# Loading the second x tile through ScalarE's DMA queue, and transposing it inside the first V group

## The chip, the cores and the metric

One core of a Trainium2 chip runs the whole kernel in one launch. The metric is the device time of an execution in microseconds (us). The *span* of a trace runs from the core's first instruction to its last; in these runs the time is the span plus 1.8 us (1.75 to 1.86), save in e13 and e17, where it is the span plus 1.83 to 2.11, for a reason that no run shows. A group of kernels measured together shares one chip and the runs of the kernel before on it; different groups ran on different chips.

The 2% that would count as faster or slower is 14 us.

## The reference, cut to what matters

A transformer block on x of 2048 x 1024 in bf16: LayerNorm, sliding-window attention of width 256 with 32 heads, then LayerNorm and a dense layer with SiLU.

```python
x = A_x
h  = x + _A_ref(_layernorm(x), A_wqkv, A_wo)      # qkv = LN(x) @ wqkv, windowed softmax, @ wo
h2 = h + _B_ref(_layernorm(h), B_w1, B_w2)        # silu(LN(h) @ w1) @ w2
return h2
```

Only the first 25 us matter to the change: LayerNorm of the first four x tiles (x0 to x3, 128 rows each) and the V projection of these rows.

## The kernel before

SyncE issues all loads in this order; each `load_wqkv` is 1 MB, each `load_x` 0.26 MB.

```python
    def load_x(b, j):
        nc.sync.dma_start(out=x_ring[(b % 2) * 4 + j], in_=x2d[(b * 4 + j) * P:(b * 4 + j + 1) * P, :])
    ...
    load_x(0, 0)
    load_wqkv(2 * D)             # V weights, columns 0 to 511
    load_x(0, 1)
    load_wqkv(2 * D + 512)       # V weights, columns 512 to 1023
    load_x(0, 2)
    load_x(0, 3)
    for c0 in (0, D, 512, D + 512):
        load_wqkv(c0)
```

A tile goes through LayerNorm on VectorE (with the root on ScalarE), is transposed on TensorE in two halves of four 128 x 128 blocks, and copied out of PSUM by ScalarE. Then a V group multiplies it: eight matmuls into one PSUM bank, and a cast of the result by ScalarE.

```python
    def turn_first(xt, dst, j):
        for h in range(2):
            for i in range(4):
                kt = h * 4 + i
                nc.tensor.transpose(out=tp_ps[h][:, i * P:(i + 1) * P], in_=xt[:, kt * P:(kt + 1) * P], identity=ident[:])
            nc.scalar.copy(out=dst[:, h * 4:(h + 1) * 4, j * P:(j + 1) * P], in_=...)
    def v_group(b, j, c, copy):
        acc = next_acc()
        for kt in range(KT):
            nc.tensor.matmul(acc, lhsT=lnT_b[b % 2][:, kt, j * P:(j + 1) * P], rhs=wv[:, kt, c * 512:(c + 1) * 512], ...)
        copy(out=v[...], in_=acc...)
    ...
    ln_first(x_ring[0], st, rs, 0)
    turn_first(x_ring[0], lnT_b[0], 0)
    ln_first(x_ring[1], st, rs, 1)
    v_group(0, 0, 0, act)
    turn_first(x_ring[1], lnT_b[0], 1)
    ln_first(x_ring[2], st, rs, 2)
    v_group(0, 1, 0, act)                 # "the second V group" below
    v_group(0, 0, 1, act)
    ...
    dummy = small.tile([P, 1], F32, name="dummy", tag="dummy")
    nc.scalar.activation(out=dummy[:], in_=eps[:], func=ACT.Exp)
```

The softmax here doesn't subtract the row's maximum and nothing guards it: scores larger than these inputs give would overflow.

## Time and profile before

| | |
|---|---|
| time known at the prediction | 699.61 us, median of 3 (699.46 to 699.77) |
| the execution that was profiled | 699.17 us, span 697.4 us |
| TensorE (PE) busy | 98% of the span |
| x1 lands | 7.28 us |
| second V group starts | 10.94 us; dense PE work from there |

The prediction below shows the lines.

### The profile page before, as it was taken

The numbers are of one execution on the slowest core, as the hardware profiler recorded it, in microseconds if no ns is written. First come the engines' busy times: TensorE is split into PE (matmuls) and PEld (weight loads), VectorE is DVE, ScalarE is ACT, GpSimd is POOL, SyncE is SP. The second block draws the span as 40 slices with busy tenths as digits, with TensorE's granted clock in tenths as the row PEclk, the third lists the DMA queues.
The fourth block names the chain that finished last, engine by engine and source line by source line (L and its number), as shares of the span: only waits on it lengthen the run. The fifth ranks groups of instructions, "written<-read, shape, count | busy, mean of one in ns | idle before, by whom it ended". The sixth has DMA issues, their size and how long they took to land.

```text
span 697.4 us, 12171 instructions
## 1 busy us (share of the span) xinstructions
PE 686.6 (98%) x4970; PEld 334.9 (48%) x5059; DVE 286.5 (41%) x608; ACT 259.9 (37%) x335; POOL 172.3 (25%) x375
## 2 busy tenths in 40 slices
PE   8999999999999999999999999999999999999998
PEld 3444555555555555544444444444444444444445
DVE  5446645753444348544425233334144251233111
ACT  4316667777777777621310023300033200233000
POOL 1006566777777777600000000000000000000000
PEclk9999999999999999999999999999999999999999
DMA  9541123025431578881023410023300024100110
GB/s 311 171 73 57 32 55 91 17 49 157 116 122 25 180 228 293 211 296 58 32 75 99 105 39 1 0 77 83 83 1 0 10 92 96 46 1 0 31 39 23
DMA packets 75399, 60.55 MB, mean 87 GB/s; under 512 B 49232, under 2 KB 59472, under 8 KB 75344
## 3 DMA queue, kind: packets, MB, share of 16 engines
q1 hardware_dynamic: 75344, 59.78, 29.7%
q8 instruction: 39, 0.64, 0.4%
q14 instruction: 16, 0.13, 0.1%
HBM read 39.85 MB, written 8.39 MB: 69 GB/s over the span
## 4 chain that ended last, share of the span: by engine, by line
PE 97%; DMA 1%; issue 1%; DVE 0%; ACT 0%; SPq 0%
PE hacc L461 18%; PE hacc L498 17%; PE acc L224 16%; PE acc L498 10%; PE acc L461 9%; PE acc L216 8%; PE acc L243 7%; PE o_ps L297 5%; PE sc L261 4%; PE hacc L243 2%; DMA r_o<-in_A_x_dram 1%; PE o_ps L196 0%; DVE ln_st L158 0%; ACT r_w L197 0%; DVE r_o L179 0%
## 5 line engine op out<-in xcount | busy, mean ns | idle before, releaser
L272 ACT ACTIVATE r_e<-sc 128x1024 bf16<-128x1024 f32 (+2 forms) x192 | 175.8, 967 | 66.1 <-PE sc L261 52.5
L287 POOL TENSOR_SCALAR_AFFINE_SELECT r_e<-r_e 128x256 bf16<-128x256 bf16 (+1 forms) x368 | 169.3, 489 | 120.7 <-ACT r_e L272 117.7
L498 PEld LDWEIGHTS <-r_a 128*128 128x128 bf16 x952 | 90.9, 98 | 103.0
L461 PEld LDWEIGHTS <-r_w 128*128 128x128 bf16 x896 | 87.4, 98 | 104.8
L498 PE MATMUL hacc<-r_a 128*128 128x512 bf16 (+2 forms) x605 | 121.9, 359 | 0.6
L461 PE MATMUL hacc<-r_e,r_w 128*128 128x512 bf16 x444 | 100.2, 379 | 0.6
L470 ACT ACTIVATE r_n<-hacc 128x512 f32<-128x512 f32 x30 | 17.9, 597 | 178.9 <-PE hacc L461 178.9
L224 PEld LDWEIGHTS <-r_w 128*128 128x128 bf16 x512 | 46.1, 98 | 58.6 <-issue 8.9
L498 PE MATMUL acc<-r_a 128*128 128x512 bf16 x328 | 73.6, 379 | 0.4
L226 DVE CAST r_a<-acc 128x512 bf16<-128x512 f32 x56 | 38.7, 691 | 81.3 <-PE acc L224 57.7
L297 PEld LDWEIGHTS <-r_e 128*128 128x128 bf16 x1440 | 50.3, 96 | 22.7
L224 PE MATMUL acc<-r_t,r_w 128*128 128x512 bf16 x240 | 60.0, 380 | 0.8
L224 PE MATMUL acc<-r_w 128*128 128x512 bf16 x246 | 57.7, 380 | 0.5
L297 PE MATMUL o_ps<-r_a,r_e 128*128 128x33 bf16 x1440 | 51.2, 178 | 0.0
L243 PE MATMUL acc<-r_o,r_a 128*128 128x512 bf16 x196 | 48.7, 380 | 0.6
L461 PE MATMUL acc<-r_e,r_w 128*128 128x512 bf16 x216 | 49.1, 379 | 0.0
L243 PEld LDWEIGHTS <-r_a 128*128 128x128 bf16 x256 | 23.1, 98 | 29.6 <-issue 5.1
L261 PE MATMUL sc<-r_a 32*128 32x128 bf16 (+2 forms) x704 | 37.2, 276 | 0.0
L513 DVE SCALAR_TENSOR_TENSOR r_t<-hacc,r_t 128x512 bf16<-128x512 f32 (+2 forms) x22 | 14.0, 635 | 56.4 <-PE hacc L498 56.4
L513 DVE SCALAR_TENSOR_TENSOR r_t<-acc,r_t 128x512 bf16<-128x512 f32 x12 | 8.3, 692 | 64.2 <-PE acc L498 59.7
L471 DVE SCALAR_TENSOR_TENSOR r_a<-r_n,hacc 128x512 bf16<-128x512 f32 x30 | 20.6, 688 | 33.0 <-ACT r_n L470 33.0
L461 PE MATMUL hacc<-r_a,r_w 128*128 128x512 bf16 x141 | 32.7, 379 | 0.2
(65 smaller groups left out, 419.7 us busy)
## 6 DMA issues: line engine op xcount, KB each, us to landing
r_w<-in_B_w_dram SPq DMA_DIRECT2D x8, 896.0 KB, 5.2
r_a<-in_B_w_dram SPq DMA_DIRECT2D x7, 1024.0 KB, 7.8
r_w<-in_A_wqkv_dram SPq DMA_DIRECT2D x6, 1024.0 KB, 11.3
r_o<-in_A_x_dram SPq DMA_DIRECT2D x16, 256.0 KB, 4.2
h_dram<-r_t SPq DMA_DIRECT2D x16, 256.0 KB, 3.2
r_t<-h_dram SPq DMA_DIRECT2D x16, 256.0 KB, 2.8
out_dram<-r_t SPq DMA_DIRECT2D x31, 128.0 KB, 1.7
r_e<-h_dram SPq DMA_DIRECT2D x3, 1024.0 KB, 5.7
```

Source lines behind the costliest of these rows:

```text
L216: nc.tensor.matmul(acc, lhsT=lnT_b[b % 2][:, kt, j * P:(j + 1) * P], rhs=wv[:, kt, c * 512:(c + 1) * 512], start=(kt == 0), stop=(kt == KT ...
L224: nc.tensor.matmul(acc, lhsT=wqk[:, kt, col0:col0 + P], rhs=lnT_b[b % 2][:, kt, :], start=(kt == 0), stop=(kt == KT - 1))
L226: copy(out=(qT, kT)[which][b][:, g, :], in_=acc)
L243: nc.tensor.matmul(acc, lhsT=qT[b][:, g, j * P:(j + 1) * P], rhs=wo[:, g, c * 512:(c + 1) * 512], start=(g == 0), stop=(g == G - 1))
L261: nc.tensor.matmul(sc[hh // 2][:, hh % 2, ch * P:(ch + nq) * P], lhsT=kT[t // 4][r0:r0 + DH, g, (t % 4) * P:(t % 4 + 1) * P], rhs=qT[b][r0 ...
L272: nc.scalar.activation(out=e[:, :, lo:hi], in_=sc[pair][:, :, lo:hi], func=ACT.Exp, scale=scale)
L287: nc.gpsimd.affine_select(out=ap, in_=ap, pattern=[[0, 2], [0, n], [sgn, P]], compare_op=ALU.is_ge if upper else ALU.is_gt, fill=0.0, base ...
L297: nc.tensor.matmul(o_ps[pair][:, qt * 2 + hh, 0:VW], lhsT=e_of(i, kind, pair)[:, hh, ch * P:(ch + 1) * P], rhs=v[:, b * 4 + kt, g * 4 + pa ...
L461: nc.tensor.matmul(acc, lhsT=w1[:, kt, ft * P:(ft + 1) * P], rhs=ln2T[b][:, kt, :], start=(kt == 0), stop=(kt == KT - 1))
L471: nc.vector.scalar_tensor_tensor(out=gT[:, ft, :], in0=th, scalar=1.0, in1=acc, op0=ALU.add, op1=ALU.mult)
L498: nc.tensor.matmul(acc[:, 0:c1 - c0], lhsT=gT[:, ft, j * P:(j + 1) * P], rhs=w2[ft // 4][:, ft % 4, c0:c1], start=(ft == 0), stop=(ft == F ...
L513: nc.vector.scalar_tensor_tensor(out=t_out[j % 2][:, c0:c1], in0=acc[:, 0:c1 - c0], scalar=0.5, in1=t_in[j % 2][:, c0:c1], op0=ALU.mult, o ...
```

## The change

Intent: get x1 to VectorE before the first megabyte of V weights, and give PE half a V group to do while x1 is normalized. A dummy Sqrt loads ScalarE's function table first.

```diff
-    def load_x(b, j):
-        nc.sync.dma_start(...)
+    def load_x(b, j, queue=nc.sync):
+        queue.dma_start(...)
...
+    eps = const.tile([P, 1], F32, name="eps")
+    nc.vector.memset(eps[:], LN_EPS)
+    dummy = const.tile([P, 1], F32, name="dummy")
+    nc.scalar.activation(out=dummy[:], in_=eps[:], func=ACT.Sqrt)
+
     load_x(0, 0)
     load_wqkv(2 * D)
-    load_x(0, 1)
+    load_x(0, 1, nc.scalar)
...
-    def v_group(b, j, c, copy):
+    def v_group(b, j, c, copy, between=None):
         acc = next_acc()
         for kt in range(KT):
+            if between and kt in between:
+                between[kt]()
...
-    v_group(0, 0, 0, act)
-    turn_first(x_ring[1], lnT_b[0], 1)
+    v_group(0, 0, 0, act, {4: lambda: turn_first(x_ring[1], lnT_b[0], 1, (0,)),
+                           6: lambda: turn_first(x_ring[1], lnT_b[0], 1, (1,))})
...
-    dummy = small.tile([P, 1], F32, name="dummy", tag="dummy")
     nc.scalar.activation(out=dummy[:], in_=eps[:], func=ACT.Exp)
```

More of the change, by code (lines that the diff above doesn't have):

```diff
@@ L123 @@
     w2_v = B_w2.rearrange("(ft p) n -> p ft n", p=P)
-    def load_x(b, j):
-        nc.sync.dma_start(out=x_ring[(b % 2) * 4 + j], in_=x2d[(b * 4 + j) * P:(b * 4 + j + 1) * P, :])
+    def load_x(b, j, queue=nc.sync):
+        queue.dma_start(out=x_ring[(b % 2) * 4 + j], in_=x2d[(b * 4 + j) * P:(b * 4 + j + 1) * P, :])
     def load_wqkv(c0):
@@ L143 @@
     make_identity(nc, ident[:])
-    eps = const.tile([P, 1], F32, name="eps")
-    nc.vector.memset(eps[:], LN_EPS)
     warm = ebuf[0]
@@ L190, in ln_first, with turn_first @@
             ln_norm(xt[:, h * 512:(h + 1) * 512], st, rs, j)
-    def turn_first(xt, dst, j):
-        for h in range(2):
+    def turn_first(xt, dst, j, halves=(0, 1)):
+        for h in halves:
             for i in range(4):
```

## The prediction

> **What bounds the kernel now.** I read the page first, for who is the bound, then the chain of waits cut to the first 40 us, then the timeline of the first 25 us, and last the DMA queue by stretches, because the change touches nothing after about 11 us.
>
> The page, busy time by engine and the chain that ended last:
>
> ```profile
> span 697.4 us, 12171 instructions
> ...
> PE 686.6 (98%) x4970; PEld 334.9 (48%) x5059; DVE 286.5 (41%) x608; ACT 259.9 (37%) x335; POOL 172.3 (25%) x375
> ...
> PE 97%; DMA 1%; issue 1%; DVE 0%; ACT 0%; SPq 0%
> ```
>
> TensorE is the bound over the whole span. Only 697.4 - 686.6 = 10.8 us of it are idle, so a change that doesn't shorten the matmuls can win only part of that. The one non-PE item of any size on the chain is "DMA", 1%. The chain of waits in the first 40 us tells where it lies (start, length, what):
>
> ```profile
> 1.73 5.55 DMA r_o<-in_A_x_dram
> 7.28 0.02 issue
> 7.30 1.30 DVE ln_st L158 x2
> ...
> 9.40 0.42 DVE r_o L179
> 9.82 0.05 issue
> 9.87 0.41 PE o_ps L196 x4
> 10.28 0.02 issue
> 10.30 0.59 ACT r_w L197
> 10.89 0.05 issue
> 10.94 3.19 PE acc L216 x14
> ```
>
> So the start is set by the second x tile (x1): issued third on SyncE's queue at 1.73, behind x0 and the first megabyte of V weights, landed at 7.28, then LayerNorm, transposes, copy, and from 10.94 on the chain is PE alone. The timeline shows the same stretch from PE's and DVE's side (start, length, engine, instruction, idle before):
>
> ```profile
> 0.80 1.28 ACT L187 ACT_TABLE_LOAD   x1 [0.80 <-PEq L535]
> ...
> 3.70 1.29 DVE L158 BATCH_NORM_STATS2 ln_st<-r_o 128x6 f32<-128x512 bf16 x2 [2.20 <-DMA r_o<-in_A_x_dram]
> ...
> 5.79 0.74 DVE L179 TENSOR_SCALAR r_o<-r_o,st_a,rs_a 128x512 bf16<-128x512 bf16 x2
> ...
> 7.30 1.29 DVE L158 BATCH_NORM_STATS2 ln_st<-r_o 128x6 f32<-128x512 bf16 x2 [0.78 <-DMA r_o<-in_A_x_dram]
> ...
> 7.33 1.90 PE L216 MATMUL acc<-r_w 128*128 128x512 bf16 x8 [0.36 <-ACT r_w L197]
> ...
> 9.87 0.72 PE L196 MATMUL o_ps<-ident,r_o 128*128 128x128 bf16 x8 [0.63 <-DVE r_o L179]
> ...
> 10.94 3.63 PE L216 MATMUL acc<-r_w 128*128 128x512 bf16 x15 [0.35 <-ACT r_w L197]
> ```
>
> Two things are to be seen. DVE is free at 5.79 + 0.74 = 6.53 and waits 0.78 us for x1: that is all that an earlier landing can give, because DVE can't start on x1 before it is done with x0. And PE idles 0.63 before the x1 transposes and 0.35 before the second V group. After that the stream is dense: 16 matmuls from 10.94 to the next transposes at 14.40 are 216 ns each; the eight transposes at 14.40 put the next group at 14.85, so eight cost 0.45 us in a dense stream.
>
> The DMA side in stretches (us, then busy of each engine, clock, DMA share, GB/s):
>
> ```profile
> 1.55:6.26 4.71, 4.25 (x11) 1.44 (x12) 2.13 (x6) 0.83 (x2) 2.08 (x1) 1.00 0.91 311
> 7.33:10.94 3.61, 2.62 (x16) 1.16 (x17) 2.37 (x6) 1.96 (x5) 0.00 (x0) 1.00 1.08 359
> 10.94:23.93 12.99, 12.88 (x70) 6.37 (x73) 4.69 (x12) 7.77 (x15) 0.00 (x0) 1.00 1.09 351
> ```
>
> The engines are saturated until about 24 us, so a second queue adds no bytes per second; it only reorders. And in the last of these stretches PE is busy 12.88 of 12.99: nothing later in the block can take back what is won before.
>
> **What the Trainium skill says.** "DMA: Bandwidth & Descriptors", section "Queues, rings and completion order": each of the 16 engines goes round its queue rows packet by packet, so x1 in its own row takes turns with V instead of standing behind it. That DMA work is bandwidth-bound here (351 to 359 GB/s) agrees with the same page's view of shared engines; that rows take turns, no view of before can show, as it has one such queue. "Perfetto Trace Analysis", section "DMA Instruction — HWDGE": the descriptor generator is shared and locked for one issue at a time, so ScalarE's issue may wait for SyncE's. Before, an unhindered issue on SyncE takes 0.40 to 0.43 us, one of an x tile at 2.83 takes 1.28, which may be such back-pressure; nothing contends yet. The same page, section "Sequencer Loop": engine instructions are pushed into a queue and others read on meanwhile. So the DMA behind the dummy Sqrt may be issued at about 1 us and not only when table load (0.80 to 2.08) and Sqrt are done; before has no case of it. "TensorE: Matmul & The Clock Gate", section "Part 1: The HAM clock gate": the clock halves after about a 3.4 us idle window. The longest gap that I foresee is under 1 us, and the granted clock of before is 1.00 in every stretch, so no clock effect.
>
> **The change part by part.**
>
> *x1's landing.* Before 7.28. Needed: by 6.5, when DVE is free. From x0 I take the plain latency: issued 0.81, landed with 3.70 at the latest, 2.9 us. If ScalarE issues at 2.3 (after table load and Sqrt, 0.20 us as the Exp dummy at 22.58 took), x1 lands uncontended at 5.2; 256 KB at half of 360 GB/s take 1.4 us in place of 0.7, so 5.9. If it issues at about 1.0 to 1.3 it lands at 4 to 5. Both are ahead of 6.5, so the exact landing doesn't matter in either.
>
> *x1's LayerNorm.* Starts at 6.5 in place of 7.30. From its start to its first transpose before was 9.87 - 7.30 = 2.57, so the first transpose now starts at about 9.07. ScalarE's root has to be at about 8.05, and ScalarE's copies of x0 end at 7.77: free.
>
> *V weights.* x1's 0.26 MB come out of the first V load's share: V landed 5.3 us after 1.27, at 6.57, and now up to 0.26 MB / 360 GB/s = 0.73 us later, 7.30. The first V group starts at 7.33 before, so this just fits; and the four matmuls ahead of the first transposes (4 x 0.216 = 0.86) need only be done by 9.07, which leaves 0.9 us of slack. The second V load and x2 have the same bytes ahead of them as before: unchanged.
>
> *PE order.* Four V matmuls 7.33 to 8.19; idle to 9.07 (0.88, worse than any one gap of before); four transposes 0.23, two matmuls 0.43, four transposes 0.23, two matmuls 0.43: 10.39. The second V group's first four matmuls need only the first half's copy, which starts near 9.5 and is done by 10.1; its second four need the second half near 11.25, copied by 10.75. So the copies, 0.59 each and 0.35 of PE idle before, are hidden. The group starts at 10.39 in place of 10.94: 0.55 us won. Of this 0.8 is the earlier LayerNorm, and 0.25 is given back because half a V group that used to run in the wait now stands behind it.
>
> *Later.* x2's transposes would come at 10.39 + 3.46 = 13.85; x2's norm ran 13.06 to 13.79 before and depends on its landing (10.95), not on PE: just in time, slack 0.1 to 0.3. From there PE is dense. The dummy Sqrt and the earlier eps memset (0.06) cost ScalarE and DVE time in which they idle.
>
> *x0.* It now may share the engines with x1 if ScalarE issues early. x0's landing heads the whole chain one for one. The DMA engines aren't full then (0.38 to 0.81 busy by stretches before 2.8 us), so I put 0.0 to 0.5 on it, 0.15 in the mean.
>
> Sum: -0.55 + 0.15 = -0.4 us, 699.61 - 0.4 = 699.2.
>
> **The rivals.**
> 1. The early issue: x1 runs abreast of x0, x0 lands up to 0.5 us later, and everything after shifts. For it: the sequencer reads on past queued work. Against it: two queues may fill the slow ramp better, and SyncE's issue is first. Time 699.4 to 699.6.
> 2. The late landing: ScalarE waits for the generator's lock while SyncE's issues are stuck (1.28 us at 2.83), or V's queued descriptors go first. The gain is gone at a landing of 7.05 and beyond it each us costs one. For it: issues of 3.4 us later in the load. Against it: V and x1 together are through by 7.28 as before. Time 699.6 to 700.2.
> 3. The whole wait vanishes: PE's 0.98 us of idle in the stretch as page readers would add it. Against it: DVE can't start before 6.5, and four matmuls no longer fill the wait. Time 698.6.
> 4. The gain is taken back: x2 becomes the wait at 13.85. Against it: it needs a landing over 0.2 us later than before. Time 699.3 to 699.5.
>
> **Range and chances.** The repeats of before spread by 0.31 us. Main branch 699.05, rival 1 and 4 699.3 to 699.6, rival 2 up to 700.2. I say 699.2, range 698.7 to 699.8. 2% is 14 us, more than the whole idle time of PE on the faster side, and no rival loses it: within 2% 0.985, faster 0.005, slower 0.01.
>
> **What would show it.** Right: x1's statistics start at about 6.5 straight behind x0's normalization with no DMA wait; one PE gap of 0.8 to 0.9 in the first V group, none before the second group, which starts near 10.4; PE dense from there and the shift unchanged at 24 us. x0's statistics still at 3.70: main branch; later: rival 1. x1's statistics waiting for DMA beyond 6.6: rival 2. A gap before x2's transposes near 13.9: rival 4. The prediction is wrong if the first x tile lands over 0.5 us later, if the time leaves 698.7 to 699.8, or if the early shift is there but the end doesn't have it.

## The result, and the profile after

The changed kernel took 698.49 us (median of 6, 698.27 to 699.01) against 699.69 us (median of 6, 699.17 to 702.72): 1.20 us between the medians. The forecast was 699.2 with a range from 698.7, so the measured time is below the range. The ratio of the fast runs is 0.9977 (95% interval 0.996 to 0.9994). Ratios here divide the mean time of one kernel's fast runs by that of the other's of the same rounds, so they are not quite the ratio of the medians, and not every ratio can be recomputed from the executions listed. This one holds an execution of before at 702.72 us, within 1.5% of the fastest and so counted as fast; without it the means are 698.53 and 699.65, a ratio of 0.9984.

The two traces differ by less than the times: spans 696.7 and 697.4 us, 0.7 apart. The timeline of the changed kernel, in the stretch that the prediction showed of before (start, length, engine, instruction, idle before):

```profile
0.80 1.28 ACT L136 ACT_TABLE_LOAD   x1 [0.80 <-PEq L539]
0.81 0.40 SPq L127 DMA_DIRECT2D r_o<-in_A_x_dram  x1
...
0.97 0.38 ACTq L127 DMA_DIRECT2D r_o<-in_A_x_dram  x1
...
3.66 1.29 DVE L161 BATCH_NORM_STATS2 ln_st<-r_o 128x6 f32<-128x512 bf16 x2 [2.16 <-DMA r_o<-in_A_x_dram]
...
6.40 1.28 DVE L161 BATCH_NORM_STATS2 ln_st<-r_o 128x6 f32<-128x512 bf16 x2
...
7.38 1.04 PE L221 MATMUL acc<-r_w 128*128 128x512 bf16 x4 [0.45 <-ACT r_w L200]
...
8.95 0.40 PE L199 MATMUL o_ps<-ident,r_o 128*128 128x128 bf16 x4 [0.53 <-DVE r_o L182]
...
9.62 0.39 PE L199 MATMUL o_ps<-ident,r_o 128*128 128x128 bf16 x4
...
9.84 4.05 PE L221 MATMUL acc<-r_w 128*128 128x512 bf16 x18
```

ScalarE issued x1 at 0.97, while its table load was still running. x1's statistics follow x0's normalization with no DMA wait, at 6.40 in place of 7.30. There is one PE gap in the first V group (0.53 us idle, where the forecast had 0.88) and none before the second. The 18 matmuls from 9.84 are the last two of the first group and the 16 of the next two, so the second V group starts two matmuls later, at 9.84 + 0.43 = 10.27 in place of 10.94. That is 0.67 us, and it is kept: the chain of waits of the changed kernel is PE alone from there.

```profile
8.48 0.42 DVE r_o L182
8.91 0.05 issue
8.95 0.40 PE o_ps L199 x4
9.35 0.43 PE acc L221 x2
9.78 0.22 PE o_ps L199 x4
10.01 3.88 PE acc L221 x18
13.89 0.45 PE o_ps L199 x8
14.34 3.45 PE acc L221 x16
```

Two questions follow: why the times differ by 1.2 when the traces differ by 0.7, and which part of the change does it.

### The profile page after: what moved, and what is told of

The parts are those of the page before. It is cut to its first block, busy times and chain, and to the rows that moved or that the text cites. A ratio compares the mean times of both kernels' runs of the same rounds, so it can differ in the third digit from the quotient of the medians.

```text
span 696.7 us, 12261 instructions
## 1 busy us (share of the span) xinstructions
PE 691.4 (99%) x5059; PEld 335.1 (48%) x5059; DVE 286.3 (41%) x608; ACT 260.0 (37%) x336; POOL 171.6 (25%) x375
## 4 chain that ended last, share of the span: by engine, by line
PE 98%; DVE 1%; DMA 0%; ACT 0%; issue 0%
PE hacc L465 19%; PE hacc L502 17%; PE acc L229 17%; PE acc L502 10%; PE acc L465 9%; PE acc L221 8%; PE acc L248 7%; PE o_ps L302 5%; PE sc L266 4%; PE hacc L248 1%; DMA r_o<-in_A_x_dram 0%; DVE ln_st L161 0%; PE o_ps L199 0%; DVE r_o L182 0%; ACT rs_a L190 0%; DVE st_a L162 0%
```

## The experiments

One relation helps to read all of them. In fourteen of the fifteen traces that run at full clock and become dense with the second V group, the span is the start of this group plus 686.4 to 686.6 us (before: 10.94 and 697.4; changed: 10.27 and 696.7). The exception is told under e12. So a tenth of a microsecond at the start is a tenth at the end, and the spans of unprofiled executions tell roughly where their second V group started.

### The kernel before again, and each half of the change alone

**e1_before_again**: no edit.

> The unchanged kernel, to get a second profile and the spread of its runs. The profiled execution of before (699.17) was the fastest of its six, the median 699.69. Theory A (the 1.2 us between the medians is the 0.68 us that the traces show in the start of the dense PE stream, and the rest is chance in which execution was profiled): a second profile shows its second V group at 10.9 to 11.4 and a span of 697.4 to 698.0, and a time over the kernel before of 1.000 within 0.0005. Theory B (before's start jitters because every delay of x1's landing goes into its path, and the change took this jitter away): its runs spread over more than 0.6 us, and x1's statistics start later than 7.30 in a slower execution.

Measured: 699.26 us (699.12 to 699.38), ratio to before 0.9997 (0.9985 to 1.001). In its trace x1's statistics start at 7.41, the second V group at 11.04, and the span is 697.5. Its own five runs spread little; the nine runs of before beside it spread from 699.18 to 699.78. Start, span and ratio are as theory A had them. Theory B's spread of over 0.6 us is not in its own runs, and is just reached in the nine.

**e2_queue_only**: the changed kernel with PE's old order.

```diff
-    v_group(0, 0, 0, act, {4: ..., 6: ...})
+    v_group(0, 0, 0, act)
+    turn_first(x_ring[1], lnT_b[0], 1)
```

> x1 through ScalarE's queue, its transposes after the first V group as before. x1 landed at 4.3, so its first half is normalized by about 8.95. The V group ends its issue at 9.1, transposes 9.1 to 9.55; the cast of the first V group stands ahead of the copies on ScalarE (9.3 to 9.9), so the first copy ends near 10.4 and the second V group starts near 10.4: gain 0.5 us of the 0.68, and the placing of the transposes is worth 0.1 to 0.2. Rival: the placing is what wins and the queue is only its condition; then this run gains under 0.2 us.

Measured: 698.98 us against 699.40 for before, ratio 0.9993 (0.9981 to 1.0006). By the medians that is 0.42 us faster, more than the rival's 0.2 (but the interval contains 1, and this kernel's buffers lie 32 bytes lower, which is told below). The second V group started at 10.83, not 10.4, mostly because x0 came late: its statistics start at 3.96 instead of 3.66 to 3.70. What the path waits for next is the cast, as the expectation had it:

```profile
7.77 1.92 PE acc L221 x8
9.68 0.02 issue
9.70 0.59 ACT r_a L223
10.29 0.50 ACT r_w L200
10.79 0.05 issue
10.83 3.63 PE acc L221 x16
```

The cast of the first V group (`r_a`) stands before the copy of the transposes (`r_w`) on ScalarE, and PE waits for both.

**e3_interleave_only**: the changed kernel with x1 back on SyncE's queue.

```diff
-    load_x(0, 1, nc.scalar)
+    load_x(0, 1)
```

> Transposes inside the first V group, x1 on SyncE's queue behind the first V load. x1 lands at 7.28, normalized at 9.82; then transposes, two matmuls, transposes, two matmuls: 0.22+0.43+0.22+0.43, so the second V group starts near 11.15, 0.2 us later than before: about 0.2 us slower than before. Rival: if the interleaving alone wins, 0.3 us faster.

Measured: 700.11 us (699.66 to 701.97), ratio 1.0008 (0.9994 to 1.0022): about 0.7 us slower by the medians, in the expected direction. (The ratio fits the other four executions; with the profiled one the means give 1.0014.) The profiled execution is the worst of its five (span 700.2). PE waits 2.02 us for x1 in the middle of the first V group, and then its granted clock falls, the share of full speed at which TensorE is let run. By stretches (us, busy of PE, its weight loads, DVE, ACT, POOL, then the granted clock, DMA share, GB/s):

```profile
9.00:10.00 1.00, 0.00 (x0) 0.00 (x0) 0.57 (x3) 0.29 (x1) 0.00 (x0) 1.00 1.09 409
10.00:11.00 1.00, 0.73 (x8) 0.50 (x9) 0.54 (x2) 0.29 (x1) 0.00 (x0) 1.00 1.04 388
11.00:15.00 4.00, 4.00 (x15) 1.64 (x14) 3.31 (x8) 1.65 (x4) 0.00 (x0) 0.57 1.09 386
15.00:18.00 3.00, 3.00 (x21) 1.62 (x20) 0.48 (x2) 1.66 (x4) 0.00 (x0) 1.00 1.09 386
```

The same trace, cut where the clock changes:

```profile
7.65:11.06 3.41, 1.39 (x12) 0.66 (x11) 2.39 (x6) 0.65 (x3) 0.00 (x0) 1.00 1.07 393
11.06:14.47 3.41, 3.41 (x13) 1.39 (x11) 2.78 (x7) 1.59 (x4) 0.00 (x0) 0.50 1.09 386
```

In the first view the column before the last two is the clock: 0.57 over 11 to 15 us. The second view shows it at half for 3.41 us, after 3.41 us in which PE was busy for 1.39. Interleaving by itself makes the longest PE gap longer, and in this execution it cost the clock as well. Its other four runs list a clock of 1.000 and spans of 697.9 to 698.5.

**e4_after_again**: the changed kernel.

> The changed kernel again, beside the others. Second V group at 10.27, x0's statistics at 3.66, span 696.7, 0.7 to 1.2 us faster than the kernel before. Theory A says nearer 0.7 to 0.9 over many runs, theory B 1.2 again, with a spread of under 0.4 us.

Measured: 698.74 us (698.67 to 698.93), 0.66 below before's median of 699.40; ratio 0.999 (0.9978 to 1.0003). x0's statistics start at 3.83, the second V group at 10.45, the span is 696.9. So the gain beside these runs is near the 0.7 of the traces, not 1.2.

### The 32 bytes

Between e1 and the others something unrelated showed: from 11 to 20 us the DMA queues moved 349 GB/s in both traces of the kernel before, and 386 in every other. The interleave-only kernel has one queue too, so it isn't the queue. What it shares with the changed kernel is the dummy tile in another pool. The pool it left had two buffers for it, so all large buffers start 32 bytes lower per partition: the weights' region at address 17408 instead of 17440.

**e5_before_aligned**:

```diff
-    dummy = small.tile([P, 1], F32, name="dummy", tag="dummy")
+    dummy = const.tile([P, 1], F32, name="dummy")
```

> The kernel before with one thing changed: the one-element dummy tile taken from the pool of constants, as the change does, which moves all big SBUF regions down by 32 bytes per partition (the weights' region from address 17440 to 17408). All runs so far with the region at 17408 moved 386 GB/s from 11 to 20 us, both with it at 17440 moved 349, whatever their queues. Theory C (the address sets the rate of the load): 386 GB/s here. If the rate matters for the time, x1 lands up to 0.3 us earlier and the kernel is up to 0.3 us faster than before; if only the issue order matters, x1 lands at 7.3 to 7.7 and the time is that of before within 0.2 us. Rival: the rate belongs to the second queue or to the early Sqrt, then 349 GB/s.

**e6_after_shifted**: the changed kernel with `pad = const.tile([P, 8], F32, name="pad")` added.

> The changed kernel with a 32-byte pad in the pool of constants, which puts the big regions back at the addresses of before (17440). Theory C: 349 GB/s from 11 to 20 us. x1 still lands near 4.3, the first V load near 7.2, x2 near 10.95 in place of 10.6, all with slack: the second V group at 10.3 to 10.5 and the time that of the changed kernel within 0.15 us. If part of the gain came from the addresses, it is 0.3 us or more slower than the changed kernel.

The stretch from 11 to 20 us, first of e5, then of e6:

```profile
11.00:20.00 9.00, 8.99 (x54) 4.63 (x55) 4.47 (x12) 5.09 (x11) 0.00 (x0) 1.00 1.09 386
```

```profile
11.00:20.00 9.00, 9.00 (x55) 4.55 (x54) 4.69 (x12) 5.23 (x12) 0.00 (x0) 1.00 1.09 350
```

The last column settles it: the address sets the rate, in both directions. What it is worth in time is not settled. e5 took 699.22 us against 699.48, 0.26 us less by the medians, ratio 0.9992 (0.998 to 1.0004), though its x1 landed at 7.35, no earlier than in before. e6 took 699.02 us, mean span 697.15; the changed kernel on the same chip (e14 below) had 697.12. So one pair says 0.26 us and the other 0.03. My expectation for e6 named x2 near 10.95; it landed at 11.46, still without a PE wait.

### The second queue or the order of the bytes?

**e8_second_on_sync**: one queue, x1 ahead of V, transposes as in the changed kernel.

```diff
     load_x(0, 0)
-    load_wqkv(2 * D)
-    load_x(0, 1, nc.scalar)
+    load_x(0, 1)
+    load_wqkv(2 * D)
```

> The changed kernel with x1 issued second on SyncE's queue, ahead of the first V load, and no DMA on ScalarE. If the gain is the order in which the bytes come and not the second queue: x0's statistics at 3.6 to 3.7 undisturbed (0.0 to 0.3 later with two queues so far), x1 lands near 4.4, V near 7.3, the second V group at 10.2 to 10.3, and the time is that of the changed kernel or up to 0.2 us faster. If the second queue itself wins something (issue time, a fuller ramp), 0.2 us or more slower than the changed kernel.

Measured: 700.61 us (699.57 to 703.58), ratio 1.0017 (0.9998 to 1.0036), against 699.48 for before. Three of its six executions, the profiled one among them, list a clock of 0.995 to 0.998 and took 701.39 us or more; the three at full clock took 699.57 to 699.83. The expectation failed: x1 came in time (statistics at 6.30), but V landed at 8.93. In the trace the engines moved almost nothing for half a microsecond once both x tiles were in, and were not full until 6.5:

```profile
3.00:3.50 0.50, 0.50 (x3) 0.15 (x1) 0.00 (x0) 0.00 (x0) 0.50 (x1) 1.00 0.96 373
3.50:4.00 0.50, 0.50 (x2) 0.15 (x1) 0.44 (x1) 0.00 (x0) 0.13 (x1) 1.00 0.30 72
4.00:6.50 2.50, 2.33 (x11) 0.83 (x10) 2.07 (x7) 0.29 (x1) 0.00 (x0) 1.00 0.86 257
6.50:8.00 1.50, 0.34 (x5) 0.26 (x5) 1.29 (x3) 1.22 (x3) 0.00 (x0) 1.00 1.04 358
```

V's issue started 0.46 us later than before (1.73 for 1.27). That alone doesn't explain the 2.36 us by which it landed later (8.93 for 6.57); the rest is open.

**e11_half_v_first**: one queue, x0, V rows kt 0 to 3, x1, V rows kt 4 to 7, transposes before matmuls 5 and 7.

> One queue only: x0, half of the first V load (kt 0 to 3, which the first four matmuls read), x1, the other half; transposes before matmuls 5 and 7. If only the order of the bytes matters: x1 has 0.5 MB less ahead of it than in before, lands near 5.9 to 6.1, x0 is undisturbed (3.6 to 3.7), the second half of V lands near 7.3 and is needed at 8.2: second V group at 10.06, span 696.5, as with the delayed issue. Against it stands the run with x1 second on SyncE, whose V load came 1.7 us late at 270 GB/s for a reason not known; if a one-queue order with an x tile ahead of V slows the queue again, V's second half lands after 8.2 and this is slower than the changed kernel.

Measured: 699.83 us (699.21 to 699.87), ratio 1.0002 (0.999 to 1.0015). The second expectation held. The second half of V arrived about 8.6, 0.3 us after PE asked for it, and x2 only at 11.88, which made x2 the wait ahead of its transposes at 14.46. Again the rate sagged, to 208 GB/s from 5.0 to 6.5 us. So a plain reordering on one queue, which moves the same bytes in a like order, doesn't give what the second queue gives. Why the single queue starves then, no run here shows.

### When ScalarE issues

My forecast called the issue time immaterial: at 1.0 or at 2.3, x1 would land before VectorE needs it. It was 0.97. To test the other instant, the dummy Sqrt writes into x1's buffer, so that the DMA must wait for it.

**e9_delayed_issue**:

```diff
-    nc.scalar.activation(out=dummy[:], in_=eps[:], func=ACT.Sqrt)
+    nc.scalar.activation(out=x_ring[1][:, 0:1], in_=eps[:], func=ACT.Sqrt)
```

> The changed kernel, but the dummy Sqrt writes into x1's buffer, so ScalarE's DMA of x1 has to wait for it and is issued at about 2.3 in place of 0.97. Over the five two-queue runs so far x0's statistics started at 3.66 to 4.29, over the five one-queue runs at 3.56 to 3.73; the second V group starts 6.61 after them in each of the changed kernel's runs. Theory D (the early issue delays x0, by 0.0 to 0.6, and this goes to the end one for one): x0's statistics are back at 3.6 to 3.7, x1 lands at 5.6 to 6.2, before DVE needs it at 6.4, the second V group starts at 10.27 to 10.35, and the span is 696.7 to 696.8 in nearly all runs, 0.1 to 0.3 less than the changed kernel's mean. Rival: the delay of x0 is chance, not contention; then nothing changes. Second rival: ScalarE's issue now waits for the descriptor generator behind SyncE's, x1 lands after 6.4 and the kernel is slower than the changed one.

**e10_delayed_split_5_7**: the same with the transposes before matmuls 5 and 7.

> The delayed issue with the transposes before matmuls 5 and 7. With the split at 5 and 7 the second V group started 6.40 after x0's statistics and not 6.61. So 10.06, a span of 696.5, 0.2 us faster than with the delayed issue alone. It is the version that the reasons point to.

Both failed badly. e9 took 700.75 us against 699.20 (ratio 1.0016, 1.0002 to 1.003), e10 702.31 (1.0041, 1.0028 to 1.0055). The chains of waits, e9 and then e10:

```profile
2.33 5.63 DMA r_o<-in_A_x_dram
7.96 0.02 issue
7.98 1.30 DVE ln_st L161 x2
```

```profile
2.33 6.83 DMA r_o<-in_A_x_dram
9.16 0.02 issue
9.18 1.30 DVE ln_st L161 x2
```

The issue itself took 0.39 and 0.40 us, so ScalarE wasn't held up by SyncE's use of the generator. The transfer then took 5.6 and 6.8 us where the changed kernel's took 3.3. What had been queued ahead by then was both V loads (issued from 1.27 to 2.31). x0 did profit: its statistics start at 3.59 and 3.49. In both traces the clock fell after PE's long gap, and every execution of e10 lists a mean clock of 0.998 or less.

**e13_issue_after_v**: x1's DMA waits for a two-column memset of its buffer on VectorE, behind the warm-up memset.

> The changed kernel, but ScalarE's DMA of x1 waits for a two-column memset of its buffer on VectorE behind the warm-up memset, so it is issued at about 1.6, behind the first V load's issue (1.26) and beside the second's. If the place in the order decides (what is issued earlier is served first, whatever its queue): x1 lands at 6.5 to 7.3 as in before, the second V group starts at 10.4 to 11.2 and the time is that of before or slower. If the two queues take fair turns, x1 lands at 5 to 6, DVE isn't kept waiting, x0 is undisturbed (3.6) and this is 0.1 to 0.3 us faster than the changed kernel.

It was issued at 1.55, after the first V load's issue began at 1.26:

```profile
1.55 5.31 DMA r_o<-in_A_x_dram
6.86 0.02 issue
6.89 1.30 DVE ln_st L162 x2
```

x1 landed at 6.86, as "the place in the order decides" had it. Issued 0.6 us later than in the changed kernel, it landed 2.6 us later. Yet the times, 698.68 us (698.62 to 699.22, ratio 0.9985, 0.9972 to 0.9997), are not those of before: the profiled execution was the slowest of the six, with a span of 697.3, and the other five had 696.6 to 696.8, so in them x1 presumably landed earlier; no trace shows it. Both halves of my expectation are met in part: the order shows in the trace, and the gain in the time is that of fair turns.

### Where the transposes stand

**e7_split_5_7** and, beside the changed kernel on the same chip, **e15_split_again**:

```diff
-    v_group(0, 0, 0, act, {4: ..., 6: ...})
+    v_group(0, 0, 0, act, {5: ..., 7: ...})
```

> The changed kernel with the transposes before matmuls 5 and 7 of the first V group in place of 4 and 6. The path is: first half of x1 normalized at 8.95, four transposes, copy (1.08 together) until 10.03, and PE has 5 matmuls ahead (until 8.46), then 0.22, 0.43, 0.22, 0.22 behind the first transposes: 10.04. So the second V group starts near 10.05 to 10.2 in place of 10.27 to 10.44: 0.2 us faster than the changed kernel. Rival: the copy of the second half comes too late for the second group's fifth matmul, then no gain.

> The split at 5 and 7 again, on the same chip as the changed kernel: second V group 6.40 after x0's statistics, mean span 0.2 us below the changed kernel's. If the mean isn't below, the 0.21 us of the single trace don't carry.

**e14_after_third** and **e18_after_fourth**: the changed kernel.

> The changed kernel a third time, for comparison on one chip. x0's statistics at 3.6 to 4.3, second V group 6.61 later, span 686.45 later: 696.7 to 697.2, and 0.6 to 1.0 us faster than the kernel before.

> The changed kernel a fourth time: mean span 696.9 to 697.1 (15 runs so far have 696.91), x0's statistics at 3.6 to 4.3, the second V group 6.61 later, the span 686.45 after that; 0.5 to 0.8 us faster than the kernel before.

| run | x0's statistics | second V group | span of this trace | time, median | ratio to before (95%) |
|---|---|---|---|---|---|
| e7 | 4.29 | 10.69 | 697.1 | 698.66 | 0.9984 (0.9973 to 0.9996) |
| e15 | 4.08 | 10.48 | 696.9 | 698.77 | 0.9986 (0.9972 to 1.0) |
| e14 | 3.88 | 10.49 | 696.9 | 698.91 | 0.9988 (0.9974 to 1.0003) |
| e18 | 4.10 | 10.71 | 697.1 | 698.85 | 0.9986 (0.9974 to 0.9999) |

The second V group starts 6.40 us after x0's statistics with the split at 5 and 7, and 6.61 with that at 4 and 6, in each trace. So the 0.21 us are real on the path. (e7 missed its 10.05 to 10.2 because x0's statistics came at 4.29.) Over the runs the mean spans on one chip are 696.91 (10 runs of e7 and e15) and 697.12 (4 runs of e14), which agrees but is too few to settle it.

**e16_queue_cast_late**: no interleaving; the cast of the first V group placed behind the copies of the transposes.

```diff
-    v_group(0, 0, 0, act, {4: ..., 6: ...})
+    held = []
+    v_group(0, 0, 0, lambda **k: held.append(k))
+    turn_first(x_ring[1], lnT_b[0], 1)
+    act(**held.pop())
```

> x1 through ScalarE's queue, transposes after the first V group as in before, but ScalarE's cast of that group placed behind the copies of the transposes. In the queue-only run the second V group started 6.87 after x0's statistics, with ScalarE busy with the cast when the copy could have begun. Without it: V group's issue ends 1.73 after its start (3.7 after the statistics), so at 5.4; eight transposes; first copy from 5.8 to 6.4; the second V group 6.5 after x0's statistics, 0.1 us earlier than in the changed kernel: the placing is then worth nothing by itself, only the order on ScalarE. If it starts at 6.8 again, interleaving is what wins.

Measured: 698.95 us, ratio 0.9988 (0.9974 to 1.0003), beside 698.91 for the changed kernel. The second V group starts at 10.76, x0's statistics at 4.11: 6.65 apart, 0.15 more than expected and 0.22 less than in e2. The chain no longer holds the cast:

```profile
7.96 1.90 PE acc L221 x8
9.86 0.24 PE o_ps L199 x4
10.09 0.02 issue
10.12 0.59 ACT r_w L200
10.71 0.05 issue
10.76 3.63 PE acc L221 x16
```

So the placing is mostly a matter of ScalarE's order: 6.65 without interleaving and 6.61 with it. In this trace the first V group also began 3.85 us after x0's statistics (7.96 - 4.11), against 3.64 in e4, as the eight transposes of x0 took 1.02 us, and 0.72 in e4; so the two may be level or the simple order a little ahead.

**e17_after_v_split**: the issue of e13 and the split at 5 and 7 together.

> The issue at 1.55 and the split at 5 and 7 together. If x1 lands as in the run with the issue at 1.55 (6.86; its unprofiled runs suggest some 0.5 earlier), its statistics start at 6.4 to 6.9 and the second V group 3.66 after them, at 10.06 to 10.55: mean span 696.5 to 696.8, 0.2 to 0.4 us below the changed kernel's beside it. If x1's landing behind the first V load is as unsteady as in before, the spread of its runs is over 0.5 us and the mean is no better.

Measured: 698.51 us (698.39 to 699.57), ratio 0.9982 (0.9968 to 0.9996), beside 698.85 for the changed kernel. Four runs have spans of 696.4 to 696.9, the profiled one 697.5, with x1 landing at 7.43. The warning in the expectation held: the landing is unsteady, and a mean span of 696.74 against 697.02 over five runs each is a candidate, not a proven better version: the mean times, 698.76 and 698.84, are closer than the spans.

### The kernel before a third time

**e12_before_third**: no edit.

> The kernel before a third time. In all one-core traces so far the span is the start of the second V group plus 686.3 to 686.6, so the spans of unprofiled runs tell where it started: before's mean span over 20 fast runs is 697.6, a start near 11.15 and x1's statistics near 7.5. Theory E (the profile that I predicted from was a fast execution with an early landing of x1): x1's statistics at 7.3 to 7.8 here, the span 686.45 later than the second V group, and this start 3.64 after the statistics. It falls if the span differs from that by over 0.2 us.

Measured: 699.43 us (699.35 to 699.75), ratio 0.9999. x1's statistics start at 7.25, earlier than I said. The second V group starts 3.63 after them, at 10.88, and the span is 697.6: 686.72 later, over my 0.2 by 0.07, so that test fell. What ends PE's waits in this trace, longest first (engine, line, waited for: us in total, times, longest):

```profile
PE sc L152 <- DVE r_e L147: 1.6, 1, 1.6
PE o_ps L196 <- DVE r_o L179: 0.9, 1, 0.9
PE acc L216 <- ACT r_w L197: 0.7, 2, 0.4
PE acc L461 <- issue: 0.2, 1, 0.2
```

The last line is a wait of 0.2 us late in the kernel (line 461 is the dense layer) that the other traces of before don't have. So the spread of before's spans is x1's landing for the larger part and late waits of this kind for some. Traces of x1 on SyncE's queue behind the first V load put its landing at 7.22, 7.28, 7.35, 7.39 and 7.69. I can't read the landing of an unprofiled run, only that its span was later.

## Why the prediction was wrong, point by point

**Right: the path.** VectorE as the limit once x1 is early (6.5 forecast, 6.40), the first transposes (9.07; 8.95), one gap in the first V group, the copies hidden, the second V group (10.39 without a delay of x0; 10.27), dense from there, no wait before x2's transposes, the shift kept to the end, no fall of the clock. The main branch's 0.55 us became 0.67 in the pair of traces. 0.04 of the difference is x0, which landed earlier than in before, and 0.08 is x1's statistics starting before x0's normalization had quite ended.

**The step that failed: the sum, "699.61 - 0.4 = 699.2".** Its gain came from one execution and its base from others. The profile, with x1 landing at 7.28 and the group at 10.94, was an execution of 699.17 us; 699.61 was the median of three with other starts. The consistent sum was to add the whole remainder to the forecast start: 10.39 + 0.15 + 686.45, plus 1.8 us from span to time, is 698.8, which is 0.3 from 698.49 and within 0.15 of e4, e14 and e18. Put in gains: I took 10.94 as the start that is improved on. Before's spans over 46 executions at full clock have a median of 697.6 (697.2 to 698.6), a start near 11.15 if all of it lies there; the changed kernel's over 20 have 696.9 (696.5 to 697.4), near 10.45. The difference of 0.7 us is what the change is worth, with what the addresses add; e4, e14 and e18 show 0.66, 0.63 and 0.70 between medians. The traces alone show less of it: three of before start the second V group at 10.88, 10.94 and 11.04, four of the changed kernel at 10.27, 10.45, 10.49 and 10.71, which is 0.47 us apart in the mean and near the 0.4 of my sum. Their spans are 0.60 apart, 0.1 of this from the late waits of e12 (0.3 us in one trace of three); that the unprofiled executions of before started later still is not shown. The 1.20 of the first comparison holds further chance: its repeats of before had two at 700.23 and 702.72.

**The range was too narrow for the same reason.** I read "the repeats of before spread by 0.31 us" from three. Over the 49 later runs they spread from 699.02 to 700.35 at full clock, and three listed a clock of 0.998 and took 701.26 to 702.27. None of the 20 runs of the changed kernel did, too few to call it a gain. That 698.49 fell below 698.7 is in part chance too: the later groups of the changed kernel, at 698.74, 698.91 and 698.85, lie inside the range.

**The term for x0 was mis-sized, and it hid behind this.** I put 0.15 us in the mean. The pair of traces showed -0.04, by luck. Nine traces with ScalarE's issue at 0.97 have x0's statistics at 3.66 to 4.29, mean 4.00; seven with one queue at 3.40 to 3.73, mean 3.61. So rival 1, the early issue that delays x0, was what happened, and costs 0.4 us on average. Its forecast of "699.4 to 699.6" was still too high, for the base again.

**A premise was wrong without harm.** "Both are ahead of 6.5, so the exact landing doesn't matter in either": e9 and e10 show that my main branch, an issue at 2.3, would have landed x1 at 8 to 9 us and made the kernel 1.5 to 3 us slower than before. I had given x1 a half share of the engines from its issue on. In the traces what counts is whether it is issued ahead of V; e13's unprofiled executions may differ. The change works because the sequencer doesn't wait for the table load, which I had down as the less welcome case.

**Rival 3** (698.6) came nearest in number and for a wrong reason: PE still idles in the first V group. **Rivals 2 and 4** didn't occur.

**Not foreseen:** the 32 bytes, which sped up the load by a tenth and the kernel by 0.03 us in one pair of runs and 0.26 in the other.

## What to carry to other kernels

Check that the execution which was profiled is the one whose time you subtract from: where a gain is tenths of a microsecond, add a forecast start to the rest of the same trace. Here a small transfer that heads a path was best issued before the large ones, and from a second queue that could be done in the first microsecond; a second queue alone didn't let it overtake. Where a part of a kernel has no slack, an early tenth at its start arrives whole at the end.

## What the Trainium skill lacked or had wrong

- "DMA: Bandwidth & Descriptors", "Queues, rings and completion order", has each engine going round its queue rows packet by packet. From that I reckoned 3.6 us for x1 beside V: a plain 2.9, with 1.4 in place of 0.7 for the bytes. Issued at 2.33 behind two queued V loads, x1 took 5.6 and 6.8 us; issued at 1.55 behind one, 5.3 and 5.9; issued at 0.97 ahead of both, 3.3 to 3.9. The page doesn't tell how far a queue that was filled first keeps its lead.
- The same page, "Issuing engines are not separate DMA queues", says that a second issuing engine only saves the sequencer's issue time. Here the order x0, x1, V on SyncE's queue alone landed V at 8.93 and made the kernel 1.1 us slower than before by the medians (0.1 to 0.4 in the three executions at full clock), while x1 from ScalarE made it 0.7 faster. The cause of the starved single queue (72 and 257 GB/s) is open.
- The same page, "How a descriptor splits into AXI transactions", lets a descriptor that isn't 256-byte aligned cost an extra transaction. The trace agrees in direction: buffers at 17408 (a multiple of 256) took 386 GB/s, at 17440 349 to 350. The page gives no such size, a tenth, for 1 KB rows, and doesn't say that it holds for the SBUF side.
- "TensorE: Matmul & The Clock Gate", "Part 1: The HAM clock gate", speaks of an idle window of about 3.4 us before the clock halves. The length agrees with e3, which is at half for 3.41 us, but the window need not be idle throughout: in e3 the longest gap is 2.02 us, and PE was busy for 1.39 of the 3.41 us before the fall (e9 1.23, e8 1.34, e10 1.50). In before and e17, windows of this length with 2.42 and 2.45 us busy let the clock stand. A later part of the page does speak of a clock that oscillates through short gaps, but gives no busy share. The other four executions of e3's kernel list a mean clock of 1.000.
- "Perfetto Trace Analysis", "Sequencer Loop", was right where I hedged: ScalarE issued the DMA at 0.97, while the table load ran from 0.80 to 2.08.
